# A fused attention, MoE and routed-expert kernel: the first chunks' scores straight from the keys, the block means as a second value product, other load layouts and a new order of steps

## The chip, the cores and the metric

The kernel runs on one core of one Trainium2 chip. The metric is the device time of one execution in microseconds; the median of three runs before the change is 538.80 (538.72 to 539.54). Engines: TensorE (PE, with its weight loads PEld), VectorE (DVE), ScalarE (ACT), GpSimd (POOL), and SyncE (SP), which issues most transfers.

## The reference, cut to what matters

Three layers one after another, all in float32. An attention with q, k, v of 2 x 8 x 768 x 64; then a dense layer with a silu gate on 1536 tokens of width 512 (hidden width 2048); then a layer of 8 experts (hidden width 1024) of which every token takes the one with the highest logit.

```python
k_sum = k.reshape(B, H, nb, 32, D).max(axis=3)
v_sum = v.reshape(B, H, nb, 32, D).mean(axis=3)
scores_l = where(|i - j| < 16, scale * q @ k.T, -1e9)
scores_s = scale * q @ k_sum.T + log(32)
a = softmax(concatenate([scores_l, scores_s], -1))
x = a @ concatenate([v, v_sum], 2)
...
h = x @ w_in;  x = (h / (1 + exp(-h))) @ w_out
...
out[t] = gate[t] * relu(x[t] @ w1[e_t]) @ w2[e_t]
```

So a query sees 31 near keys and the 24 block maxima of the keys; its values are the near values and the 24 block means.

## The kernel before, in words

The 1536 tokens are six chunks of 256 (`c`), four head pairs each (`hp`); chunks 0 to 2 are the first batch. A chunk's queries go in four tiles of 64, and a tile's window is 96 keys and 24 block entries, 120 columns (`KW` = 96, `NC` = 120). Everything is issued from one list of step names, `STEPS` (lines 60 to 89): a letter names a step, a digit its chunk, and each occurrence takes the next head pair or block; a mark behind it names the engine (`'` VectorE, `*` ScalarE, `_` GpSimd). Each engine runs its own instructions in that order and waits for data and buffers by semaphores, and SP's loads stand in SP's queue in the same order.

The steps of the opening: `k` loads keys (transposed, padded) and `K` takes block maxima on VectorE; `q`, `v` load queries and values; `n`, `Z`, `M` load values by rows, sum their blocks on TensorE (L205) and scale them to means on VectorE (L227, into `vsum`). `W0`, `W1` (`windows`, lines 315 to 323) are GpSimd's: for chunks 0 and 1 three copies build the 120-column tile `a` out of the keys and the maxima. `D` (`dots`, lines 325 to 342) makes the scores on TensorE, eight products a step; where `windows` has made a tile, each product reads all 120 columns (L339), and the branch behind it (L341, L342) is not used. `T` masks and takes maxima on VectorE (L355), `E` exponentials on ScalarE (L361), `R`, `N` the normalisation (L365 to L370), `P` turns on TensorE (L376), `C` copies the turned weights. `A0`, `A1` (`add_means`, line 301) copy the means into rows 96 to 119 of the value tile on GpSimd; `V` (`values`, line 388) is eight products over 120 rows (L395); `H`, `L` split the result into a high part and a rest (L399, L403). Later chunks load ready key windows (`load_step`).

Weights of the dense layer come as 64-bit words: `l` loads a block of 128 columns (`load_raw`, L236 and L238), `a` is two operations on ScalarE (L248, L250), `b` and `c` integer operations on VectorE (L254, L258), `h` the high part (L170, a helper that copies) and `p` the rest (L276) on VectorE. `F` is 24 matmuls of the hidden layer (L414; `F0` to `F3` are quarters of it, six each), `t`, `u` the gate, `g`, `w` its split, `G` twelve matmuls of the second product (L451). Raw blocks, keys and rows of values share one tag of 16 buffers.

Routing: `i`, `r`, `e` pick an expert, rank the tokens and write a table to DRAM; `plan` and `prow` lay out work units (a count on TensorE, L578, and some forty small VectorE operations); `read` loads the table rows by an indirect DMA of GpSimd (L730); `ids` turns them on TensorE (L739). Experts: `ga` gathers rows, `f1`, `f2` load 1 MB of weights, `1h`/`1r`, `2h`/`2r` split them, `f` and `z` are the two products (L911, L905, L901; L963, L957, L951), `ym` scales, `yo` writes.

```python
copy(by, k[:, :, :QT], t[:, o:o + CH].rearrange("p (g k) -> p g k", g=G))
...
nc.tensor.matmul(ps[:, :NC], q[d, t + i], k[d, t + i], start=True, stop=True)
...
nc.tensor.matmul(ps[d, t], v[:, t, d], r[:, 2 * h + t // 2, t % 2 * QT:(t % 2 + 1) * QT], start=True, stop=True)
```

## Time and profile before

| | |
|---|---|
| median of 3 runs | 538.80 us |
| the profiled execution | 540.28 us |
| its span in the trace | 538.5 us |
| TensorE busy | 512.5 us, 95% |
| VectorE, ScalarE, GpSimd busy | 394.0, 227.6, 77.8 us |
| moved by the DMA engines | 77.37 MB |

The span is the time between the first and the last instruction of the profiled execution. A busy engine is not one at its peak: TensorE has two clock levels, 1.2 and 2.4 GHz, and the profile gives the granted clock of a stretch as a share (0.50 and 1.00). In a row of the timeline the first number is the start and the second the time from the start of the first to the end of the last of the instructions that are merged in it. What stands in brackets is the idle time of the engine before them and what ended it. TensorE's instructions overlap, so the price of a step is read from its start to the start of the next.

### The profile page before, as it was taken

The page shows a single profiled execution, that of the slowest core. Times are in us where ns is not written, and L with a number is a line of the kernel's source. Part 1 is how long each engine was busy: PE and PEld are TensorE (multiplying, and loading weights), DVE is VectorE, ACT ScalarE, POOL GpSimd, SP SyncE. Part 2 cuts the span into 40 slices and gives each one's busy share as a digit, 9 for nine tenths or more (in the row PEclk, how much of TensorE's full clock was granted, in tenths as well). Part 3 has the DMA queues.
Part 4 walks back from the last instruction along what each step waited for, and adds up shares of the span by engine and source line. Part 5 has one row for each costly group of instructions (what it writes and reads, how often), then busy time and mean ns, then how long its engine had stood idle before and what let it go on. Part 6 is the DMA issues. An engine that isn't in the chain of part 4 may idle for free. (4 is left out here: it accounts for less than half of the span.)

```text
span 538.5 us, 10109 instructions
## 1 busy us (share of the span) xinstructions
PE 512.5 (95%) x3716; PEld 425.1 (79%) x3716; DVE 394.0 (73%) x1058; ACT 227.6 (42%) x548; POOL 77.8 (14%) x110
## 2 busy tenths in 40 slices
PE   6979999999999999999999997999989999899992
PEld 3569888988988888889898987898957867687671
DVE  5889999996878768486768684769857656993650
ACT  4879996763433344243140302233224341233330
POOL 4440001000010000011003114010340202110021
PEclk8879999999999999999999998999989999999998
DMA  8997637064562202221010109110084659965430
GB/s 310 316 288 250 204 100 243 6 198 144 173 239 84 98 28 45 85 84 44 1 55 2 39 1 338 55 40 1 31 273 175 209 204 331 306 243 194 157 125 30
DMA packets 42986, 77.37 MB, mean 144 GB/s; under 512 B 3905, under 2 KB 17832, under 8 KB 42930
## 3 DMA queue, kind: packets, MB, share of 16 engines
q1 hardware_dynamic: 38322, 66.92, 38.1%
q0 software_dynamic: 2592, 6.33, 3.3%
q10 hardware_dynamic: 2016, 3.40, 1.7%
q8 instruction: 31, 0.51, 0.4%
q14 instruction: 25, 0.20, 0.1%
HBM read 87.28 MB, written 6.67 MB: 174 GB/s over the span
## 5 line engine op out<-in xcount | busy, mean ns | idle before, releaser
L414 PE MATMUL h<-x,wi 128*128 128x256 f32 x1152 | 146.9, 286 | 0.0
L414 PEld LDWEIGHTS h<-x,wi 128*128 128x128 f32 x1152 | 141.6, 192 | 2.0 <-issue 0.8
L451 PE MATMUL x<-wo,g 128*128 128x512 f32 x576 | 142.1, 399 | 0.0
L451 PEld LDWEIGHTS x<-wo,g 128*128 128x128 f32 x576 | 105.7, 188 | 24.5 <-issue 1.0
L863 DVE TENSOR_TENSOR sp<-r,sp 128x512 fp32r<-128x512 f32 x112 | 72.4, 686 | 23.3 <-ACT sp L170 22.6
L424 ACT ACTIVATE t<-h 128x512 f32<-128x512 f32 x48 | 28.5, 596 | 68.3 <-PE h L414 62.7
L911 PE MATMUL jh<-xTT,sp 128*128 128x256 f32 x384 | 50.3, 286 | 0.0
L911 PEld LDWEIGHTS jh<-xTT,sp 128*128 128x128 f32 x384 | 47.6, 191 | 3.0 <-issue 2.0
L963 PE MATMUL jy<-sp,jT 128*128 128x512 f32 x192 | 49.8, 407 | 0.0
L361 ACT ACTIVATE a<-a,m 128x120 f32<-128x120 f32 x96 | 36.8, 387 | 27.8 <-DVE m L355 27.8
L492 DVE CUSTOM_DVE_ANT_0 dull<-row,gate 128x512 bf16<-128x512 f32 x64 | 44.4, 693 | 1.4
L170 ACT CAST sp<-r 128x512 fp32r<-128x512 f32 x65 | 36.9, 619 | 16.3 <-DMA r<-w 6.1
L963 PEld LDWEIGHTS jy<-sp,jT 128*128 128x128 f32 x192 | 35.9, 192 | 9.9 <-issue 1.2
L427 DVE SCALAR_TENSOR_TENSOR t<-t,h 128x512 f32<-128x512 f32 x48 | 32.8, 683 | 14.8 <-ACT t L424 14.6
L435 DVE TENSOR_TENSOR g<-t,g 128x512 fp32r<-128x512 f32 x48 | 32.7, 690 | 9.3 <-ACT g L170 8.7
L355 DVE CUSTOM_DVE_ANT_0 a<-s,mask 128x120 f32<-128x120 f32 x96 | 21.3, 278 | 14.6 <-PE s L339 14.5
L170 ACT CAST g<-t 128x512 fp32r<-128x512 f32 x30 | 18.2, 618 | 23.0 <-DVE t L427 19.1
L563 POOL DMA_INDIRECT tbl<-tb,ix x12 | 13.3, 1112 | 100.8 <-DVE cum L555 83.0
L920 ACT ACTIVATE jT<-jh 128x512 fp32r<-128x512 f32 x16 | 9.6, 599 | 33.4 <-PE jh L911 25.2
L170 DVE CAST sp<-r 128x512 fp32r<-128x512 f32 x47 | 19.6, 432 | 4.1 <-PE jy L963 1.8
L399 ACT CAST x<-o 128x256 fp32r<-128x256 f32 x24 | 8.6, 368 | 29.2 <-PE o L395 28.6
L170 POOL COPY v<-vsum 24x512 f32<-24x512 f32 x15 | 13.1, 900 | 52.3 <-DVE vsum L227 36.4
(210 smaller groups left out, 651.0 us busy)
## 6 DMA issues: line engine op xcount, KB each, us to landing
r<-w SPq DMA_DIRECT2D x28, 1024.0 KB
rm<-w SPq DMA_DIRECT2D x32, 512.0 KB
...
```

Source lines behind the costliest of these rows:

```text
L170: (nc.scalar.copy if by is nc.scalar else by.tensor_copy)(dst, src)
L355: nc.vector.tensor_tensor_reduce(a[:, j], ps[j // 2][:, j % 2, :NC], mask[:, v], -0.125, 3.0e38, ALU.add, ALU.min, m[:, 0, j:j + 1])
L361: nc.scalar.activation(a[:, t], a[:, t], AF.Exp, bias=m[:, 0, t:t + 1], scale=-1.0, accum_out=m[:, 1, t:t + 1])
L414: nc.tensor.matmul(hs[c, p][:, j], wi[p][:, u, k, j * P:(j + 1) * P], xt[c, k][:, v], start=(j + k + n == 0), stop=(j == 1 and k == KB - 1 ...
L424: nc.scalar.activation(t, hs[c, p], AF.Tanh, scale=0.5)
L427: nc.vector.scalar_tensor_tensor(ts[c, p], ts[c, p], 1.0, hs.pop((c, p)), op0=ALU.add, op1=ALU.mult)
L435: by.tensor_tensor(g[:, 1], ts.pop((c, p)), g[:, 0].bitcast(F32), op=ALU.subtract)
L451: nc.tensor.matmul(x2p[c][i], g[:, v, j, i * P:(i + 1) * P], wo[f][:, u], start=(f == 0 and n == 0), stop=(f == FB - 1 and n == 2))
L492: nc.vector.tensor_tensor_reduce(dull, r, gates[e], 1.0, 0.0, ALU.mult, ALU.add, lg[:, i * E + e:i * E + e + 1])
L863: by.tensor_tensor(dst[:, 1], src, dst[:, 0].bitcast(F32), op=ALU.subtract)
L911: nc.tensor.matmul(hps[i, p][:, j], sp1[p // 2 * 4 + k][:, u, f:f + P], x[v][:, k], start=(k + n == 0), stop=(k == 3 and n == 2))
L963: nc.tensor.matmul(yps[i, t], h[:, v, j, t * P:(t + 1) * P], sp2[2 * p + j][:, u], start=(p + j + n == 0), stop=(p == 3 and j == 1 and n = ...
```

## The change

Chunks 0 and 1 no longer build a window tile. `windows` and its steps go; `dots` takes the branch with two products: 96 columns straight from the loaded keys, then 24 columns from the block maxima. `A0` and `A1` go too: `values` makes two accumulating products for these chunks, one over the value tile and one over the means, both over 120 rows, where the value tile holds zeros in rows 96 to 119 and `vsum` zeros in rows 0 to 95 (one GpSimd memset). Their value loads come from a new array padded to 128 rows (`vn2`), so 256 KB instead of 192. Blocks of `w_in` are stored so that each partition's 4 KB lie in one run, where before four runs of 1 KB were read. All steps of all stages stand in a new order, and some of them run on another engine; outside of `W0`, `W1`, `A0`, `A1` their numbers are the same.

```diff
--- before.py
+++ after.py
 STEPS = """
-k K W1 k K q1 D1 T1 E1 W0 k q0 D0 k K q0 W0 T0 E0 D0 T0 l a K W0 W0 q0 R0 D0 T0 q0 D0 E0 E0 W1 W1 q1 D1 N0 P0 b T0 n Z E0 n Z c R0 R0 R0 h* n R1 Z N0 C0* N0 P0 p P0
-W1 T1 M A1_ A0_ l l a a l a l N0 C0* P0 q1 D1 A1_ A1_ A0_ b b N1 a q1 D1 C0* C0* c c T1 A1_ v0 v0 V0 V0 v0 A0_ b E1 h* H0 L0 H0 L0 v0 A0_ h* R1 E1 v1 V0 v1 H0 c h*
-P1 p F0 F0 l l N1 l C1* a V0 H0 P1 C1* L0 F0 T1 E1 p b a L0 c V1 V1 v1 v1 F0 H1 H1 R1 q2 p F1 F1 F1 F1 t l R1 N1 a a P1 C1* N1 P1 l b t C1* a L1 F3 A2_ L1 F3 u V1 V1
...
-u g' w u i T5 L5 x* d3 d3 d3 d3 r g' t E5 R5 G w V5 N5 d3 d3 d3 d3 e e G u g* P5 C5' H5 d3 d3 L5 G V5 H5 L5 F w F G t t d3 d3 x* d3 d3 u d3 d3 i r u g' w F rt rc* rt
-g* w F e e rl rc' rl i t G u tiles g' w t u g' r w G plan prow f1 F t u g' G w F t u g* w e e e e e read ids ga F t f2 2h' 2r f2 u ga ga 2h* 2h* F t 2h* u g* w 2r
...
+k k K K q0 q0 q0 D0 D0 T0 k K E0 T0 D0 T0 n k K E0 R0 R0 q1 Z E0 N0 l a D1 T1 b R0 q0 D0 T0 E1 P0 C0* n Z n Z q1 D1 E0 c h* N0 R0 N0 N0 q1 l l M P0 a b a P0 P0 p C0*
+C0* C0* l b a v0 V0 v0 v0 H0 V0 H0 D1 T1 c q1 D1 v0 V0 V0 h* R1 b L0 L0 T1 E1 R1 E1 p F0 F0 H0 H0 N1 P1 N1 l L0 a v1 L0 c P1 h* C1* F0 l l l F0 c h* v1 C1* T1 E1 b
+R1 t V1 V1 p p F1 F1 F1 F1 N1 R1 N1 H1 L1 v1 H1 a L1 u a a l P1 C1* F3 b l P1 C1* F3 V1 b v1 V1 l l c c c F2 t u a b b H1 F2 L1 F2 H1 L1 F2 q2 q2 c c h* l l F3 l l
+F3 g* w g* h* h* h* t a p p G t w u A2_ b a a D2 u p p g' w G g* G c h* h* T2 p a p F F a a w b b b G b c c a c c E2 t u l l h* h* h* h* p p p R2 p b F F N2 P2 g* w
...
+T5 E5 R5 N5 d3 d3 d3 d3 C5* d3 F t u g* P5 C5' V5 w H5 L5 G V5 H5 L5 F t G i r x* e e e rt rc' F rt t u e e g' tiles u g* rc' w w F t F G u g' w t u g* i r e rl e rl
+i F r w F t u g* e plan prow f1 t G G 1h* e read F f2 2h* f2 u F ids ga ga ga ga g' w w t u g' G G G 1h' 1r lt lt 2h' w G 2h* t u 1r 2h* 2r 1h' 1r g* w G lc' ls lc'
...
@@ -95,7 +95,7 @@
 
 
 @with_exitstack
-def fused_kernel(ctx: ExitStack, tc, qw, kw, kt, vw, vr, vt, w_in, w_out, w_gate, w1, w2, masks, blocks, items, out):
+def fused_kernel(ctx: ExitStack, tc, qw, kw, kt, vw, vn2, vr, vt, w_in, w_out, w_gate, w1, w2, masks, blocks, items, out):
     nc = tc.nc
     cp = ctx.enter_context(tc.tile_pool(name="const", bufs=1))
     dr = ctx.enter_context(tc.tile_pool(name="dram", bufs=1, space=DRAM))
@@ -224,6 +224,8 @@
 
         ps = vsum[b]
         vsum[b] = cp.tile([NC, DM], F32, tag="vsum", name=f"vsum{b}")
+        if b == 0:
+            nc.gpsimd.memset(vsum[b][:KW], 0.0)
         nc.vector.tensor_scalar_mul(vsum[b][KW:NC], ps[KW:NC].rearrange("p a b -> p (a b)"), 1.0 / BLOCK)
 
     wi, wo = {}, {}
@@ -233,7 +235,7 @@
     def load_raw(kind, f):
         pool = wp.tile([P, DM], I64, tag="wo", name=f"raw{kind}{f}", bufs=FB) if f < ROOMY else st.tile([P, DM], I64, tag="stage", name=f"raw{kind}{f}")
         if kind == "i":
-            nc.sync.dma_start(pool.rearrange("p (k f) -> p k f", k=KB), w_in[:, f * P:(f + 1) * P].rearrange("(k p) f -> p k f", p=P))
+            nc.sync.dma_start(pool, w_in[f])
         else:
             nc.sync.dma_start(pool, w_out[f * P:(f + 1) * P])
         raws[kind, f] = pool
@@ -289,14 +291,17 @@
         for hp in range(HP):
             qs[c, hp] = q[:, hp].rearrange("p a b -> p (a b)")[:, :CH].rearrange("p (g q) -> p g q", g=G)
             rr[c, hp] = q[:NC, hp]
-            vs[c, hp] = v[:NC, hp]
+            vs[c, hp] = v[:, hp]
             ws[c, hp] = a[:, hp]
 
     def load_q(c, hp):
         nc.sync.dma_start(qs[c, hp], qw[c, hp])
 
     def load_v(c, hp):
-        nc.sync.dma_start(vs[c, hp][:KW], vw[c, hp])
+        if c < 2:
+            nc.sync.dma_start(vs[c, hp], vn2[c, hp])
+        else:
+            nc.sync.dma_start(vs[c, hp][:KW], vw[c - 2, hp])
 
     def add_means(c, hp, by=nc.vector):
         copy(by, vs[c, hp][KW:NC], vsum[c // 3][KW:NC, hp * P:(hp + 1) * P].unsqueeze(1).to_broadcast([NB, G, P]))
@@ -311,16 +316,6 @@
 
     def add_sums(c, hp, by=nc.vector):
         copy(by, ks[c, hp][:, :, KW:NC], ksum[:, c // 3, hp:hp + 1].to_broadcast([P, G, NB]))
-
-    def windows(c, hp, by=nc.gpsimd):
-
-        b, g = divmod(c, 3)
-        k = ks[c, hp] = ws[c, hp]
-        o = CH * g
-        t = kts[b, hp]
-        copy(by, k[:, :, :QT], t[:, o:o + CH].rearrange("p (g k) -> p g k", g=G))
-        copy(by, k[:, :, QT:KW], t[:, o + QT:o + QT + CH].rearrange("p (g k) -> p g k", g=G)[:, :, :KW - QT])
-        copy(by, k[:, :, KW:NC], ksum[:, b, hp:hp + 1].to_broadcast([P, G, NB]))
 
     def dots(c, hp):
 
@@ -392,7 +387,12 @@
         for t in range(G):
             for h in range(2):
                 d = slice(h * D, (h + 1) * D)
-                nc.tensor.matmul(ps[d, t], v[:, t, d], r[:, 2 * h + t // 2, t % 2 * QT:(t % 2 + 1) * QT], start=True, stop=True)
+                w = r[:, 2 * h + t // 2, t % 2 * QT:(t % 2 + 1) * QT]
+                if c >= 2:
+                    nc.tensor.matmul(ps[d, t], v[:, t, d], w, start=True, stop=True)
+                    continue
+                nc.tensor.matmul(ps[d, t], v[:NC, t, d], w, start=True, stop=False)
+                nc.tensor.matmul(ps[d, t], vsum[0][:, hp * P + h * D:hp * P + (h + 1) * D], w, start=False, stop=True)
 
     def x_high(c, hp):
         x = xt[c, hp] = xp.tile([P, 2, CH], F32R, tag="x" if c else "g", name=f"x{c}{hp}", bufs=XBUFS - 4 if c else 4)
@@ -1070,7 +1070,7 @@
     }
     for c in range(NCH):
         steps = [(c, hp) for hp in range(HP)]
-        for x, f in zip("qvWDTERNPCABVHL", (load_q if c < 2 else load_step, load_v, windows, dots, lows, exps, shares, norm, turn, keep, add_means, add_sums, values, x_high, x_rest)):
+        for x, f in zip("qvDTERNPCABVHL", (load_q if c < 2 else load_step, load_v, dots, lows, exps, shares, norm, turn, keep, add_means, add_sums, values, x_high, x_rest)):
             todo[f"{x}{c}"] = each(f, steps)
     todo["A2"] = each(lambda *a: (add_sums(*a), add_means(*a)), [(2, hp) for hp in range(HP)])
     for n in range(4):
@@ -1097,7 +1097,7 @@
 
 
 
-_NAMES = ["qw", "kw", "kt", "vw", "vr", "vt", "w_in", "w_out", "w_gate", "w1", "w2", "masks", "blocks", "items"]
+_NAMES = ["qw", "kw", "kt", "vw", "vn2", "vr", "vt", "w_in", "w_out", "w_gate", "w1", "w2", "masks", "blocks", "items"]
 
 
 def _arrays(q, k, v, moe_w_in, moe_w_out, moe2_w_gate, moe2_w1, moe2_w2):
@@ -1161,8 +1161,8 @@
     it[:, 200:232] = moe2_w_gate.reshape(KB, P, E).transpose(1, 0, 2).reshape(P, KB * E)
     it[:, 320:448] = np.triu(np.ones((P, P)), 1)
     return dict(
-        qw=qw.reshape(NCH, HP, P, G, QT), kw=kwn.reshape(NCH, HP, P, G, NC)[2:], kt=kp, vw=vwn.reshape(NCH, HP, KW, G, P), vr=vr, vt=vt,
-        w_in=con(moe_w_in).view(np.int64), w_out=con(moe_w_out).view(np.int64), w_gate=con(moe2_w_gate.T),
+        qw=qw.reshape(NCH, HP, P, G, QT), kw=kwn.reshape(NCH, HP, P, G, NC)[2:], kt=kp, vw=vwn.reshape(NCH, HP, KW, G, P)[2:], vn2=np.pad(vwn.reshape(NCH, HP, KW, G, P)[:2], ((0, 0), (0, 0), (0, P - KW), (0, 0), (0, 0))), vr=vr, vt=vt,
+        w_in=con(moe_w_in.reshape(KB, P, FB, P).transpose(2, 1, 0, 3)).view(np.int64).reshape(FB, P, DM), w_out=con(moe_w_out).view(np.int64), w_gate=con(moe2_w_gate.T),
         w1=con(moe2_w1), w2=con(moe2_w2), masks=masks, blocks=blocks, items=it)
 
 
```

## Rows read from the trace of the kernel before

**Rows 1.** The page, part 1: busy time, share of the span, instructions.
```profile
PE 512.5 (95%) x3716; PEld 425.1 (79%) x3716; DVE 394.0 (73%) x1058; ACT 227.6 (42%) x548; POOL 77.8 (14%) x110
```
**Rows 2.** Timeline of TensorE, opening: start, length in us, then what.
```profile
6.50 0.64 PE L339 MATMUL s<-a,q 64*64 64x120 f32 x16 [1.06 <-POOL a L170]
...
28.85 1.03 PE L395 MATMUL o<-q,v 120*64 120x64 f32 x16 [1.68 <-POOL v L170]
...
33.18 2.85 PE L414 MATMUL h<-x,wi 128*128 128x256 f32 x12
...
50.40 5.78 PE L451 MATMUL x<-wo,g 128*128 128x512 f32 x24
```
**Rows 3.** Timeline of TensorE, steady stretches at full clock.
```profile
62.49 5.76 PE L451 MATMUL x<-wo,g 128*128 128x512 f32 x24
...
163.43 0.69 PE L395 MATMUL o<-r,v 120*64 120x64 f32 x16
164.04 0.64 PE L339 MATMUL s<-k,q 64*64 64x120 f32 x16
164.61 3.12 PE L414 MATMUL h<-x,wi 128*128 128x256 f32 x24
...
173.94 0.60 PE L376 MATMUL t<-ident,a 128*120 128x128 f32 x4
174.30 5.95 PE L414 MATMUL h<-x,wi 128*128 128x256 f32 x48
```
**Rows 4.** Stretches: PE, PEld, DVE, ACT, POOL busy; PEclk, DMA share, GB/s.
```profile
10.00:18.00 8.00, 6.61 (x70) 4.61 (x64) 6.54 (x36) 7.22 (x33) 3.52 (x10) 0.50 1.08 374
16.00:18.00 2.00, 2.00 (x5) 0.97 (x4) 1.90 (x13) 1.93 (x9) 0.14 (x1) 0.50 1.13 355
20.00:22.00 2.00, 2.00 (x6) 0.90 (x5) 0.90 (x9) 1.61 (x3) 0.00 (x0) 1.00 1.07 367
22.00:28.00 6.00, 4.53 (x62) 2.80 (x61) 5.08 (x6) 5.16 (x15) 4.27 (x5) 1.00 1.06 228
30.00:36.00 6.00, 4.63 (x34) 4.38 (x34) 5.96 (x23) 5.08 (x15) 1.41 (x2) 0.51 1.05 283
```
**Rows 5.** Timeline of VectorE, opening.
```profile
22.89 0.70 DVE L227 TENSOR_SCALAR vsum<-vm 24x512 f32<-24x512 f32 x1 [1.99 <-PE vm L205]
...
24.20 2.12 DVE L254 SCALAR_TENSOR_TENSOR rawi<-rawi,three 128x512 int32<-128x512 int32 x2
...
32.44 0.68 DVE L276 TENSOR_TENSOR wi<-rawi,wi 128x512 fp32r<-128x512 f32 x1
...
43.04 1.41 DVE L254 SCALAR_TENSOR_TENSOR rawo<-rawo,three 128x512 int32<-128x512 int32 x2
```
**Rows 6.** Timeline of TensorE, routing.
```profile
316.74 0.18 PE L578 MATMUL cnt<-cum,ones 128*128 128x8 bf16 x1
...
329.03 0.37 PE L739 MATMUL entp<-ident,ents 4*128 4x4 f32 x2 [3.52 <-DMA ents<-tbl,rix]
329.32 7.53 PE L414 MATMUL h<-x,wi 128*128 128x256 f32 x48
```
**Rows 7.** Timeline of TensorE, experts: the two pauses and the last matmuls.
```profile
400.12 1.10 PE L901 MATMUL jh<-rm,xT 128*64 128x512 f32 x4 [2.18 <-DVE xT L170]
401.15 2.93 PE L963 MATMUL jy<-sp,jT 128*128 128x512 f32 x6
...
460.44 0.65 PE L926 MATMUL hp<-ident,hr 128*128 128x128 f32 x4 [1.50 <-ACT hr L916]
...
525.83 3.07 PE L957 MATMUL iy<-sp,hT 128*128 128x512 f32 x12
```
**Rows 8.** Timeline of POOL, opening: the copies of the means.
```profile
23.73 7.68 POOL L170 COPY v<-vsum 24x512 f32<-24x512 f32 x8 [7.59 <-DVE vsum L227]
```
**Rows 9.** The chain that ended last: one of five short matmuls in a row.
```profile
359.17 0.03 PE lo L541
```
**Rows 10.** The chain that ended last: a weight load of the experts.
```profile
449.51 9.69 DMA r<-w
```

More of the change, by code (lines that the diff above doesn't have):

```diff
@@ L76 @@
-1h' 1r G 1h' g* 1r 1h' 2r w 1h' f1 1h* 1h' G 1h* lt lt 2h* 2h' lc' ls 2r lc' 2r G G G x* rt rc* 1r 1r 1r ls f 2r f1 rt f f lt rl rc* rl 1r 1r f rh f f 2h' i rr r 1h*
-1r z 2r f f rh cn pl f pl pl pl pl pl f rr pl 1h* 1r lc' f st ls 1h* pl pl pl pl pl 1r 1h* 1h* ga lt lc' pl pl pl pl pl pl f rh pl pl f f f f1 pl f2 pl pl f z 2h' 2r
-z z rh rr z z 2h* 2r pl rr z pl pl 2h* 1r 1h' 1r z ls f pl pl pl pl pl 1h* 1h* pl pl f f f pl 1r pl f2 pl ex 2h* 2h' rh 2h* f f ex 1h* f f 1r 1r 2h' 2h' 2h' rr e ex
@@ new lines @@
+G C2' V2 H2 A2_ g* t w u L2 D2 l a b c h' p l a g' b c h' G G p F F T2 E2 R2 N2 l a l a t t b c h' p w j b c q3 P2 H2 C2* G h* u L2 p u V2 H2 L2 F g' J B3_ w g* j j
+G F t t F w j G u q3 J B3* D3 t D3 J J g' x* w G m s u u m s T3 F g' w E3 R3 m m N3 P3 G s s Y O d0 d0 T3 E3 R3 t u g* d0 d0 d0 w M F t A3* C3' u g' w g' F q3 V3 H3
+L3 B3_ q3 D3 B3_ G t T3 E3 G d0 d0 N3 P3 F R3 N3 d0 d0 d0 u P3 A3_ A3* C3* V3 H3 w C3* d0 d0 d0 F L3 q4 B4_ q4 q4 A3* g' t u t V3 H3 g* w w D3 L3 T3 E3 R3 N3 q4 G G
+P3 B4' u g* G d0 C3' d0 w D4 T4 E4 D4 T4 R4 N4 d0 i V3 H3 G x* q5 q5 L3 F t u g' w F t u d1 F F d1 d1 d1 t d1 A4* r P4 C4* A4' g' G w G u t u g* g* e E4 w V4 H4 d1
@@ new lines @@
+d1 L4 B4_ D4 F R4 N4 P4 d1 d1 d1 C4* T4 E4 R4 B4_ t u G V4 D4 F w T4 E4 t N4 P4 G d1 d1 B5_ D5 C4' u H4 L4 R4 A4' V4 T5 E5 g' g* N4 w F t R5 N5 G d1 d1 x* d1 B5_ w
+P4 d1 d2 d2 d2 d2 d2 H4 L4 u C4* A4* F A5_ t u g' i G P5 V4 H4 L4 F t w G C5* V5 d2 d2 g* D5 d2 A5' w G F F T5 E5 q5 A5_ B5* d2 d2 d2 d2 u g* w D5 G t t u d2 d2 q5
+B5* d2 d2 u x* d3 F g* w t d3 d3 d3 g' w G G T5 E5 u g* d3 w r F t d3 R5 N5 u F g' w P5 C5' F R5 N5 t u H5 L5 d3 d3 d3 d3 t u V5 D5 g* H5 L5 G G w G A5* d3 P5 g* w
+T5 E5 R5 N5 d3 d3 d3 d3 C5* d3 F t u g* P5 C5' V5 w H5 L5 G V5 H5 L5 F t G i r x* e e e rt rc' F rt t u e e g' tiles u g* rc' w w F t F G u g' w t u g* i r e rl e rl
@@ new lines @@
+i F r w F t u g* e plan prow f1 t G G 1h* e read F f2 2h* f2 u F ids ga ga ga ga g' w w t u g' G G G 1h' 1r lt lt 2h' w G 2h* t u 1r 2h* 2r 1h' 1r g* w G lc' ls lc'
+f1 1h' 1h' 1h* ls f 2r 2h* 2r 2r 1r 1r 1r x* rt rc* rt rc* 2h* 2r 2r f f rl rl i lt lt lc* ls f rh r rr 1h* 1h* 1r 1r f f f f f rh rr cn pl f1 f f f rh f f f f pl pl
+pl pl pl 1h' 1h' 2h* pl pl f1 pl pl pl pl pl pl pl pl 1h* pl z z 2r pl 1h* 1h* lc' 1h* st pl pl pl pl pl pl pl pl pl pl pl pl ls f2 z z 2h* 2r f2 1r rr z z pl pl pl
+pl 1r 1r 1r 1r 2h* pl pl 2h* ex ex ex f f rh rr f f rh rr 1r ex ex ex ex ex ex z ym* f 1h* ex f1 m1 m1 f e e 1h' f 1h* rd tw f rh rr f it ic 2h* ga 2h' z 2r 2r 2r 2r
@@ new lines @@
+z z z 1h* lt 1h' f2 ga ga lt 1r 1r 1h' f f f ym' f rh 2h' 2h' 1r 1r mga mga f f 1r z lc' lc* m1 f ls ls rr f1 1h' m1 1h' 1h* rh 1r 1h* f1 f 2r mlt mlc' f f f mf 2h*
+2h' 2h* rr mf mf mf ga mrh mga 2h' 2h' 2h* 2r 2r 2r 2r 2r z 1r 1r 2r lt mht 1r z 1r rh z rr f2 2h* 2r m2 m2 2r 2h' mhc* ga f f f f1 1h' ga 1r 1h' m2 ym' lc* f rh f z
+f rr f 1h' f 1r ls rh f 1r f 2h' mlt 2h* 1h* mz mz m2 mz mz m1 ym' m1 m1 m1 mlc' f2 rr 1r 2r f1 mlt mlc' f 2r z z f 1h* 1h* 1r 2r 1h' 1r 1r f f rh rr 1h' lt lt f f
+1h' z lc' 1h' 1h' 1h* yo 1r 1r mf mf f2 lc' ls ls mf mf mrh z m2 2h' 2h' 2r f f 2h* 2r 1r mht mhc* m2 m2 2h* mym* yo yo mga m2 lt 1r f f lc* f1 z z 2h* 1h* 1h' ls 1r
@@ new lines @@
+1r f1 z z f 2r 2r rh 1h' 1h' 1r 1r f f f f rh ht 1h* mz mz mz hc* mz mym* ht 1r f f rr rh f rh z z ht hc' rr 1h' 1h' z z ym* myo 2h' yo 1r 1r 1r myo f m1 1h' 1r f
+ym* 2h' 2h* f f 2r ht hc' f2 2h' m1 m1 2r 2r 2r rr 2h' yo 2h' 2h' z z 2r 2r 2r mf mf hc* yo rr 2r m1 mf mf f1 1h* 1h' 1h' 1h* z z z f1 1r 1r mrh f2 ga mht m2 2h* m2
+2r 2h' 2r f2 lt 2h* 2h' z rh rr mhc' 2h' 2h' 2r 2r z f f f z z z lc* ls f rh 2h' 2h' m2 m2 mz mz mz mz 1r mlt mlc' 1r 1h' 1h' 2r 2r z z f f f rr 1h* f2 2r 2r mym* f
+1r 1r 1r m1 1h* 1r 2h* 2h* 2h* 2r rh rr f f f f f1 1h* 1h* 1h' z z 2h* f2 2h* f f f 2r f 1r 2h' z z 2h' f 1r f ym* ym' rh rr rh z z ht yo m1 mf m1 m1 mf m2 mf mf mrh
@@ L89 @@
+m2 2r 2r z 2r mht 2h* f2 2h* 2h' 1h' 1r 2r f hc' 1r f mhc' 2r 2r z rh ht ym' rr hc* rr m2 m2 yo mz 2r mz mz mz mym' yo myo myo 2h* 2r z z z z 2h' 2r 2r z z z z ym'
+yo ym* yo
 """
```

22 lines of the change are left out of this document (2 added, 20 removed).

## The prediction, made before the change was run

> **What bounds the kernel now.** I read the page first: TensorE is busy for 95% of the span [rows 1], so the question at every stage is where TensorE pauses or runs at its lower clock, and what work is added to it. Its own timeline shows three kinds of loss.
>
> The opening. The first scores start at 6.50, after a POOL copy; the value products stand still for POOL's copies of the block means; the hidden layer (L414) starts at 33.18; the first pair of second products (G, L451) at 50.40 [rows 2]. The work that TensorE does up to there, at the steady prices of later stretches: a value step takes 0.61 from its start to the next, a scores step (16 records) 0.57, a turn 0.36, and 48 hidden matmuls 5.95, or 0.124 each [rows 3]. The block sums are 12 records at about 0.40, since five weight loads fit into the 2 us from 20 on [rows 4]. So 8 x 0.57 + 12 x 0.40 + 8 x 0.36 + 8 x 0.61 + 96 x 0.124 = 4.6 + 4.8 + 2.9 + 4.9 + 11.9 = 29.1 us of work end at 50.4. Some 21 us are lost, nearly all before 33.2: no pause stands in the timeline after that, only a stretch at clock 0.51 [rows 4]. What ends the loss is VectorE. It waits 1.99 for the block sums, then its integer operations take 1.06 each while POOL copies, against 0.70 later, and so the rest of the second weight block, which the first hidden matmul needs, comes at 32.44 [rows 5].
>
> The routing stage. TensorE counts the tokens at 316.74, and it stands still for 3.52 until the table has been read back at 329.03; the next 48 hidden matmuls take 7.53 [rows 6] instead of 5.95, as the clock has fallen. That is 3.5 + 1.6 = 5.1 us.
>
> The expert stage. One pause of 2.18 with six matmuls after it that take 2.93 [rows 7], twice the steady time (24 in 5.76 [rows 3]), so 1.5 more, and one pause of 1.50. The last matmul ends at 528.90 [rows 7] and 9.6 us of writing follow.
>
> **The change, part by part.** *Taken from POOL:* eight window steps of three copies each and eight copies of the means, these in a row of 7.68 us [rows 8]. They lie ahead of TensorE's pauses, so this is where the opening can shrink. POOL gets one memset of the means' first 96 rows; it is idle there, and even at the 0.96 of a copy [rows 8] it is done long before VectorE writes the means.
>
> *Added to TensorE:* 64 score products of 24 columns and 64 value products of 64, two records each. No row shows a 24-column product of this shape. From below, bare short matmuls go through at 0.03 us each [rows 9]: 128 x 0.03 = 3.8. From above, a 120-column record takes 0.57 / 16 = 0.036: 4.6. I take 4.4, since weight loads come with each. The second value products have the shape of the first, 8 x 0.61 = 4.9; if two accumulating products on the same columns overlap less than the alternating ones, I allow half as much again, 7.3. Together 9.3, from 8.7 to 11.9. The Trainium skill (TensorE: Matmul & The Clock Gate, section "Wait — 56ns, not 53.3ns?") says that starts of small matmuls never lie closer than about 25 ns; by that figure the short score products would cost an estimated 3.2 instead of 4.4, and the time would come out 1.2 us lower. The nearest rows, with weights of this shape, speak for more.
>
> *New waits:* the second score product waits for VectorE's block maxima, as POOL's third copy did. Behind it in TensorE's queue stands only the next scores step, so it costs at most one reduction that VectorE does anyway. Reading the keys where they lie holds their four buffers until the last scores step of chunk 1; the weight tag has 16 buffers, and 11 loads are issued by then, so no load waits.
>
> *Loads:* ahead of the first value load stand one weight block and one query block fewer, 0.65 MB, 1.8 us at the 367 GB/s of the stretch from 20 to 22. While the 96-row value loads flow, the rate falls to 228 GB/s [rows 4]. Four loads of 262 KB at 367 take 2.9 us, four of 197 KB at 228 took 3.4. If the padded loads stay at 228, they take 4.6. Either way the values are there before the first value step. The weight blocks in one run per partition: a stretch full of the old blocks moved 355 GB/s and the next one 367 [rows 4], so four of them come at most 0.2 us sooner. I count nothing, for VectorE's work hides it; without that cover it is those 0.2 us.
>
> *The order, opening.* Ahead of the first hidden part TensorE has 8 x 1.12 + 4.8 + 4 x 0.36 + 4 x 1.22 = 20.1 us; from a start at 5.9 (0.6 earlier, without the copy) that ends at 26.0 if nothing pauses. VectorE has two integer operations and a normalisation less ahead of it, some 2.1 us at 0.70 each, is no longer slowed (4 x 0.36 = 1.4) and need not wait for the sums (up to 2.0, half of it taken): 33.2 - 2.1 - 1.4 - 1.0 = 28.7, which I take. From there to the first G come 4 x 1.22 + 4 x 0.36 + 11.9 = 18.2 of work. In the old order that stretch was 17.2 long with 5 value steps, 3 turns and the hidden matmuls, 16.0; with its loss of 1.2 again, the first G starts at 48.1, or 2.3 earlier with the same work behind it. VectorE is not late there any more: it has nine operations of 128x512 fewer before that point than in the old order (four rests, a join, a sign, two gatings, one g rest), 9 x 0.70 = 6.3. Ends: 26.0 + 18.2 = 44.2, a gain of 6.2; and, at 11.9 for the added products and TensorE at the low clock wherever it was low before (10 to 18 and 30 to 36 [rows 4], 14 us, half of it lost), 53.8, a loss of 3.4.
>
> *The order, middle.* From the first G to the routing TensorE hardly pauses; the steps between a hidden block and its second product leave 7.5 us or more of other matmuls in the new order, so it stays full: 0.
>
> *The order, routing.* From the count to the table's return pass 329.03 - 316.74 = 12.3 us. The new order puts G G F F between the two, 2 x 2.88 + 2 x 2.98 = 11.7, where F G F stood. The pause shrinks to 0.6, and with so short a one the clock stays: 5.1 - 0.6 = 4.5 gained. Ends: 0, if VectorE reaches the plan late, and 5.1.
>
> *The order, experts and end.* The same work; most distances grow (the first activation to its second product from 1.6 us of matmuls to 8.8), some shrink: the weights of the last job's second half must be split within 1.8 us of matmuls after their buffer comes free. Up to 5.2 can be gained (2.2 + 1.5 + 1.5) and as much lost. I take 0. The last writes stay at 9.6.
>
> **Sum.** 2.3 + 4.5 = 6.8 us. The profiled execution took 540.28 (its span 538.5 and 1.8 around it), so it becomes 533.5; the median shown, 538.80, lies 1.5 below that execution and becomes 532.0.
>
> **The rivals.** (a) *The opening packs fully*: TensorE never pauses after 5.9, 6.2 + 4.5, so 528.1. For it: the new order leaves no engine behind another. Against: VectorE, ScalarE and TensorE then have nearly equal loads, and each handover costs. (b) *The routing pause stays*: VectorE's queue stands before the plan, 538.8 - 2.3 = 536.5. (c) *The experts give it back*: one more pause of the 2.18 kind with its slow matmuls (3.7) and the opening at no gain, 538.8 - 4.5 + 3.7 = 538.0. This also holds the case that the change does not do what it says: POOL's copies leave, but VectorE alone set 33.18. (d) *Slower, by the experts' weights*: a load took 9.69 us to land [rows 10], and the new order leaves between 1.8 and 6.4 us from a free buffer to the split in four places. ScalarE and VectorE split in order, so what stands behind the split stops too. Two such waits of 5 us that TensorE cannot cover make 538.8 - 6.8 + 10 = 542.0; it decides from 6.8 us of new pauses on. Against it: the old order had a distance of 1.4 and TensorE did not pause there. (e) *Slower, by the clock*: the opening's TensorE has no slack now, so each us at 1.2 GHz costs half of one. From (50.4 + 4.5 - 44.2) x 2 = 21 us on the change loses; 27 us would give 541.6. Rows at about 0.50 covered 14 us before, when TensorE was mostly waiting. The Trainium skill (TensorE: Matmul & The Clock Gate, "What's actually happening") says that the clock is low by default and activity frees it; no row shows the denser opening, and by that rule (e) is the less likely.
>
> **How the numbers follow.** Forecast 0.43, (a) 0.14, (b) 0.13, (c) 0.12, (d) 0.10, (e) 0.08. Less than 0.2%, 1.1 us, can't be told from no change. Faster is the forecast, (a) and (b): 0.70. Same is (c): 0.12. Slower is (d) and (e): 0.18. The range runs from 527.5, just under (a), to 540.0: it holds (b), (c) and the bounds of the added products, and leaves out (d) and (e).
>
> **What would show it.** Right: no POOL copy before 35 us; first scores near 5.9; first hidden matmul at 28 to 29.5, first G near 48; integer operations of 128x512 at 0.70 in the opening; under 1 us of pause before the table's return and no low clock after it. Wrong: a first G later than 50.4, clock 0.50 over most of 8 to 35, a pause over 3 us before the table, or new pauses of TensorE behind weight loads after 400.

## The result, and the profile after

The kernel after takes 526.14 us in the median of 4 runs (525.14 to 526.83) against 538.76 before (538.24 to 539.54): a ratio of 0.9763, interval 0.9743 to 0.9783, 12.6 us less. The forecast was 532.0 in a range that began at 527.5. The direction was right and nearly half of the gain was not foreseen. The two profiled executions, 540.28 and 526.15, lie 14.1 apart, for the one before lay 1.5 above its median.

The page's first part, after (before: [rows 1]):

```profile
PE 506.1 (97%) x3972; PEld 425.3 (81%) x3972; DVE 400.6 (76%) x1075; ACT 217.0 (41%) x527; POOL 66.5 (13%) x83
```

TensorE has 256 records more and is busy 6.4 us less: part of its busy time before was time at the low clock. Up to the last matmul the granted clock stood at 0.50 for 23.9 us before and for 3.4 us after. Its timeline in the opening (before: [rows 2]):

```profile
6.23 0.42 PE L336 MATMUL s<-kt,q 64*64 64x96 f32 x8 [1.36 <-DMA q<-qw]
...
22.55 0.34 PE L394 MATMUL o<-q,v 120*64 120x64 f32 x4
...
24.61 0.42 PE L336 MATMUL s<-kt,q 64*64 64x96 f32 x8
...
25.20 0.42 PE L336 MATMUL s<-kt,q 64*64 64x96 f32 x8
...
28.16 1.69 PE L414 MATMUL h<-x,wi 128*128 128x256 f32 x12
...
46.36 2.97 PE L451 MATMUL x<-wo,g 128*128 128x512 f32 x12
```

The first hidden matmul came at 28.16 (before 33.18), the first second product at 46.36 (before 50.40), and between 22.55 and 46.36 no pause is listed. Two value steps with both products lie between 22.55 and 24.61, so 1.03 each against 0.61 for one product [rows 3]. A scores step with both products takes 25.20 - 24.61 = 0.59, against 0.57 with one [rows 3]. The stretches (columns as in [rows 4]):

```profile
10.00:18.00 8.00, 7.69 (x78) 4.06 (x79) 5.87 (x33) 6.44 (x28) 0.00 (x0) 0.79 1.05 394
...
22.00:28.00 6.00, 6.00 (x195) 5.70 (x196) 5.59 (x27) 5.68 (x20) 0.00 (x0) 1.00 1.03 402
28.00:34.00 6.00, 6.00 (x100) 5.70 (x98) 5.97 (x20) 5.69 (x19) 0.00 (x0) 1.00 1.04 402
```

No POOL work (the fifth pair), no low clock after 18, and transfers at 402 GB/s where 228 went. VectorE's integer operations take 0.75 each (before 1.06 [rows 5]):

```profile
20.89 0.75 DVE L256 SCALAR_TENSOR_TENSOR rawi<-rawi,three 128x512 int32<-128x512 int32 x1
...
27.55 0.66 DVE L278 TENSOR_TENSOR wi<-rawi,wi 128x512 fp32r<-128x512 f32 x1
```

The routing (before: [rows 6]) and the experts (before: [rows 7]), TensorE's timeline:

```profile
314.01 0.18 PE L578 MATMUL cnt<-cum,ones 128*128 128x8 bf16 x1
...
325.51 0.40 PE L739 MATMUL entp<-ident,ents 4*128 4x4 f32 x2
...
339.49 2.83 PE L451 MATMUL x<-wo,g 128*128 128x512 f32 x11 [0.41 <-DVE g L435]
...
439.02 3.76 PE L905 MATMUL jh<-sp,xT 128*128 128x512 f32 x15 [1.30 <-ACT hr L916]
...
507.99 5.86 PE L957 MATMUL iy<-sp,hT 128*128 128x512 f32 x24
```

From the count to the table's turning TensorE now works for 11.5 us without a pause. In the experts 1.30 and a 0.31 are left of 3.7 us of pauses, and the granted clock stays at 1.00 up to the last matmul. The last one ends at 513.85, 15.05 earlier than before; the writing behind it takes 10.45 (before 9.6).

### The profile page after: what moved, and what is told of

Its sections match the earlier page's. It is cut to its first block, busy times and chain, and to the rows that moved or that the text cites. A ratio compares the mean times of both kernels' runs of the same rounds, so it can differ in the third digit from the quotient of the medians.

```text
span 524.3 us, 10579 instructions
## 1 busy us (share of the span) xinstructions
PE 506.1 (97%) x3972; PEld 425.3 (81%) x3972; DVE 400.6 (76%) x1075; ACT 217.0 (41%) x527; POOL 66.5 (13%) x83
## 4 chain that ended last, share of the span: by engine, by line
PE 61%; issue 21%; DVE 8%; DMA 5%; POOL 3%; ACT 1%; SPq 0%; POOLq 0%; DVEq 0%
PE h L414 24%; PE x L451 22%; PE jh L911 4%; PE jy L963 3%; PE o L392 2%; POOL out L977 2%; DVE sp L863 2%; PE s L334 2%; DMA r<-w 2%; PE t L371 1%; DMA vn<-vr 1%; DMA v<-vn 1%; DMA q<-qw 1%; POOL out L974 1%; PE lo L515 1%
## 5 line engine op out<-in xcount | busy, mean ns | idle before, releaser
L414 PE MATMUL h<-x,wi 128*128 128x256 f32 x1152 | 144.0, 282 | 0.1
L414 PEld LDWEIGHTS h<-x,wi 128*128 128x128 f32 x1152 | 139.1, 188 | 2.2 <-DVE x L403 0.3
L424 ACT ACTIVATE t<-h 128x512 f32<-128x512 f32 x48 | 28.7, 597 | 66.5 <-PE h L414 55.6
L963 PE MATMUL jy<-sp,jT 128*128 128x512 f32 x192 | 48.1, 398 | 0.0
L170 ACT CAST sp<-r 128x512 fp32r<-128x512 f32 x54 | 31.4, 619 | 39.6 <-DMA r<-w 25.4
L170 DVE CAST sp<-r 128x512 fp32r<-128x512 f32 x58 | 22.9, 420 | 21.1 <-DMA r<-w 14.2
L170 POOL COPY k<-ksum 128x96 f32<-128x96 f32 x12 | 6.1, 511 | 182.7 <-DMA k<-kw 144.0
L170 ACT CAST g<-t 128x512 fp32r<-128x512 f32 x27 | 16.7, 620 | 26.5 <-DVE t L427 16.3
L977 POOL DMA_INDIRECT out<-y,ids x11 | 12.7, 1153 | 61.6 <-ACT y L968 34.4
```

The source lines that it names most:

```text
L170: (nc.scalar.copy if by is nc.scalar else by.tensor_copy)(dst, src)
L414: nc.tensor.matmul(hs[c, p][:, j], wi[p][:, u, k, j * P:(j + 1) * P], xt[c, k][:, v], start=(j + k + n == 0), stop=(j == 1 and k == KB - 1 ...
L424: nc.scalar.activation(t, hs[c, p], AF.Tanh, scale=0.5)
L963: nc.tensor.matmul(yps[i, t], h[:, v, j, t * P:(t + 1) * P], sp2[2 * p + j][:, u], start=(p + j + n == 0), stop=(p == 3 and j == 1 and n = ...
L977: nc.gpsimd.indirect_dma_start(out=outs[j][:, :], out_offset=bass.IndirectOffsetOnAxis(ap=ids[:, j:j + 1], axis=0), in_=ys.pop((i, t)), in ...
```

## The experiments

Besides the forecast's reason (each stage gains what its own pause was) there were rivals: the order gives everything; the new code and loads give it; the gain hangs on the products' price. "Before" was run again beside each group, at 538.9 to 539.5 in the median.

**The order and the code, each alone.** The first is the kernel before with the new list of steps; `W0`, `W1` stand behind the maxima and `A0_`, `A1_` behind `M`.

```diff
-k K W1 k K q1 D1 T1 E1 W0 k q0 D0 ...
+k k K W0 K W0 q0 q0 q0 D0 D0 T0 k K W0 E0 ...
...
+M A0_ A0_ A0_ A0_ A1_ A1_ A1_ A1_ P0 ...
```

> The kernel before with the new order alone: GpSimd still builds the windows (each right after the block maxima of its head pair) and still copies the means (right behind their scaling); old loads. My theory (the new order closes the routing's and the experts' pauses by itself, some 8.5 us; its opening needs TensorE and VectorE free of GpSimd's copies): 538.8 - 8.5 and up to 3 lost in the opening, so 530 to 533, with the first pair of second products no earlier than 50. Rival A, the order gives all of it and the code next to nothing: 526 to 528. Rival B, the gain comes from the code and the loads: 537 to 539.

Measured: 527.40 us, ratio 0.9771 (0.9737 to 0.9804). Its opening:

```profile
9.91 1.17 PE L339 MATMUL s<-a,q 64*64 64x120 f32 x16 [1.57 <-POOL a L170]
...
25.05 1.34 PE L395 MATMUL o<-q,v 120*64 120x64 f32 x32 [1.11 <-DMA v<-vw]
...
47.93 3.46 PE L451 MATMUL x<-wo,g 128*128 128x512 f32 x12
```

POOL's copies are there and TensorE waits for them, yet the first second product comes 2.5 us sooner than in the profile before. Rival A holds: the order gives some 11.5 of the 12.6 us, and the two intervals overlap. My theory that the new opening needs POOL's copies gone falls.

The other half, the kernel after with the old list less `W0`, `W1`, `A0_`, `A1_`:

> The kernel after with the old order (less the steps that no longer exist). My theory: the pauses of 3.5 us at the table and of 2.2 and 1.5 us in the experts are back; in the opening GpSimd's 4.3 us of waits go against some 3.4 us of added products and VectorE's old queue, so 536 to 539. By the forecast's prices of the added products (9.3 us): 541 to 544. Rival B (code and loads): 527 to 530.

Measured: 538.81, ratio 1.0003 (0.9977 to 1.0029), as my theory had it. The new code in the old order gains nothing:

```profile
28.91 0.28 PE L393 MATMUL o<-q,v 120*64 120x64 f32 x2 [1.90 <-issue]
...
50.10 5.76 PE L450 MATMUL x<-wo,g 128*128 128x512 f32 x24
...
328.18 0.37 PE L738 MATMUL entp<-ident,ents 4*128 4x4 f32 x2 [3.06 <-DMA ents<-tbl,rix]
```

The table's pause is back, and the first second product is 0.3 earlier than before. There is a new kind of pause: 1.90 us in the middle of a value step, between two equal records, for which the profile shows no releaser.

**The order in two parts, on the new code.** One kernel has the new order up to `ids` and the rest in the old one, the other the old order up to the first `G` and the rest in the new one.

> The kernel after with its own order up to the turning of the table's rows, and from there what is left in the old order. If the new order of the expert stage is worth what TensorE's lost time there says (it grows by some 5.5 us more before than after): 530.5 to 533, with pauses of 2.2 and 1.5 us again. Rival: those pauses came from where the earlier stages had left the loads and buffers, so they do not return: 526 to 527.5.

> The kernel after with the old order up to the first second product and from there what is left in the new order. If the opening's gain is the code's (no copies of GpSimd): 526 to 527.5. If it is the new order's: 526.1 + 4.4 = 530.5, between 529 and 532, with the first second product at 49 to 51.

Measured: 535.03 (0.9885 to 0.9974, runs from 531.75 to 539.71) and 531.95 (0.9801 to 0.9885; first second product at 51.24). The first lies above both of its branches, the second just inside the 529 to 532 of the order. Both profiles have the mid-step pause, 2.54 and 2.17 us. The first has besides a new pause where the old list takes over, for the gathered rows:

```profile
335.75 0.66 PE L870 MATMUL xp<-ident,xgq 128*128 128x128 f32 x4 [2.31 <-DMA xgq<-x2d,ids]
```

In its experts there are pauses of 0.78 and 1.29, smaller than the 2.2 and 1.5 expected. What a stage's order is worth can't be read from such a kernel, so the split was made again on the kernel before, whose TensorE has fewer instructions there.

**The order in parts, on the kernel before.** First a single exchange in the old list:

```diff
-... e e e e e read ids ga F t f2 ...
+... e e e e e read F t ids ga f2 ...
```

> The kernel before with one exchange in its order: the turning of the table's rows (and the first gather behind it) stands behind the next 48 hidden matmuls instead of in front of them. By the forecast's working (the pause of 3.5 us and the low clock's 1.6 after it are covered by 5.95 us of matmuls): 538.9 - 5.1 = 533.8, between 533 and 535. Rival (the gather and the rows' turning come later by as much and TensorE waits there instead): 537 to 539, with a pause of 2 us or more at the first turned rows.

Measured: 534.92, ratio 0.9934 (0.9908 to 0.9960), so 4.1 us by the medians.

```profile
315.79 0.18 PE L578 MATMUL cnt<-cum,ones 128*128 128x8 bf16 x1
...
328.10 0.40 PE L739 MATMUL entp<-ident,ents 4*128 4x4 f32 x2 [0.69 <-DMA ents<-tbl,rix]
...
338.15 0.63 PE L871 MATMUL xp<-ident,xgv 128*128 128x128 f32 x4 [0.56 <-DMA xgv<-x2d,ids]
```

The pause shrinks from 3.52 to 0.69, and the next link, the gathered rows, takes 0.56 back. The forecast's routing term is confirmed within half a microsecond, the rival (all of it waits at the gather) is not.

Then the opening alone, and everything from `plan` on alone:

> The kernel before (its products, copies and loads) with the new order only up to the first second product, and what is left in the old order. If the new opening is worth what the order-alone kernel's trace says (the lost time at 63 us is 17.1 there and 19.7 before): 538.9 - 2.6 = 536.3, between 535.5 and 537.5. If the opening's gain needs the direct scores and second value products: 538 to 539.5.

> The kernel before with the old order up to the plan and the new order for what is left (routing's second half, the rest of the dense layer, the experts). If the late part of the order carries the routing's 4.1 (as the late turning of the table's rows alone gave) and the experts' 5: 529 to 531. If the experts' pauses only disappear where the stages ahead are new too: 533.5 to 535.

Measured: 539.38 (0.9987 to 1.0032) and 530.07 (0.9822 to 0.9880). The late part carries 9.0 us. Less the 4.1 of the exchange, the experts' new order is worth 4.9, and the ratios' intervals of the two kernels (0.9908 to 0.9960, 0.9822 to 0.9880) lie apart. This counts as the experts' whatever else differs from `plan` on; the routing differs little, for a pause of 1.41 is left ahead of the table here, and 0.69 and 0.56 were left with the exchange. From 349 on its timeline lists no pause at all, and from 395 to 405 TensorE is full, where it stood at clock 0.83 before (busy for 7.68 us of 10):

```profile
395.00:405.00 10.00, 10.00 (x59) 6.69 (x58) 9.44 (x18) 3.64 (x7) 6.26 (x5) 1.00 0.58 184
```

The new opening, with the order up to `plan`, gives 2.7 us on top of the new late part (530.07 to 527.40). On top of the old one the new opening gives nothing: the 535.5 to 537.5 of my expectation is missed, and the time lies in the other branch, though the copies are there in the order-alone kernel too. In this kernel the first second product comes 2.1 earlier than in the profile before, at 48.34, but later TensorE stands still longer:

```profile
328.50 0.37 PE L739 MATMUL entp<-ident,ents 4*128 4x4 f32 x2 [3.87 <-DMA ents<-tbl,rix]
...
405.83 3.32 PE L901 MATMUL jh<-rm,xT 128*64 128x512 f32 x6 [2.56 <-DMA rm<-w]
```

Why the old late part gives the opening's gain back was not tried further; this profile also fell on one of its longer runs (542.55). And the place of the first second product in one profile is a rough measure: with the exchange and with the new late part the opening's code and order are those of before (50.40), and it stands at

```profile
49.46 5.78 PE L451 MATMUL x<-wo,g 128*128 128x512 f32 x24
...
48.74 5.79 PE L451 MATMUL x<-wo,g 128*128 128x512 f32 x24
```

So differences under some 1.7 us in it show nothing, and of the 2.1 here little may be real. The 46.36 of the kernel after lies clear of all three.

**One part of the change undone.** Four kernels have the new order and all of the new code but one part: GpSimd's windows back (`windows` and `W0`, `W1`); GpSimd's means back (`A0_`, `A1_`, one value product, 96-row loads); 96-row loads alone; the old layout of `w_in`. A fifth has both copies back with the new loads.

```diff
-            nc.sync.dma_start(vs[c, hp], vn2[c, hp])
+            nc.sync.dma_start(vs[c, hp][:KW], vn2[c, hp, :KW])
...
-            nc.sync.dma_start(pool, w_in[f])
+            nc.sync.dma_start(pool.rearrange("p (k f) -> p k f", k=KB), w_in[:, f * P:(f + 1) * P].rearrange("(k p) f -> p k f", p=P))
```

(The third and the fourth kernel; in the third, GpSimd zeroes rows 96 to 127 once.)

> The kernel after, but GpSimd builds the windows of chunks 0 and 1 again, so the scores are one product of 120 columns (each window right after the block maxima of its head pair; the four of chunk 1 behind the last maxima). Theory now (the order gives nearly all; a second score product of 24 columns costs about 0.02 us a step, 0.2 in all, and GpSimd's copies delay the first scores by up to 2 us that later work mostly hides): 526.5 to 527.5. By the forecast's price (4.4 us for the second score products): 522 to 524. If the direct scores carry the code's gain: 527.5 to 529.

> The kernel after, but chunks 0 and 1 take their block means from rows 96 to 119 of the value tile, copied there by GpSimd right behind the means' scaling, in one value product, with value loads of 96 rows. Theory now: 64 value products fewer give back some 3.2 us of TensorE, and GpSimd's copies and the slower loads take 1 to 3: 524.5 to 527. Rival (the copies' wait is what the second products were made for and costs as much as before, 3.2 us and VectorE slowed): 527 to 529.

> The kernel after with value loads of 96 rows for chunks 0 and 1 (rows 96 to 127 are zeroed once by GpSimd at the start); everything else as it is. If the padded loads matter (96 rows go at 228 GB/s where 128 rows go at 402, so the loads ahead of the first values and weights come up to 2 us later): 527 to 528.5, with the first value step later than 22.9. If transfers are hidden in the opening: 525.8 to 526.5.

> The kernel after with the old layout of w_in, four runs of 1 KB per partition for each block. My forecast's bound (0.2 us at most): 526.0 to 526.5. Rival (the loads set the opening, full at 400 GB/s from 10 to 34 us): 527 or more, the rate of the weight blocks' stretches below 380 GB/s.

> New order and new loads, but the products of before: GpSimd builds the windows and copies the means (each copy right behind its value load). It is the order-alone kernel plus the new layouts, or the kernel after without its second products. Theory now (the code's part of the gain is the loads, 2 to 3 us each in the kernels that undo one; second products and copies cost about the same): 525 to 527. If the second products are what the gain over the order alone (1.3 us) comes from: 527 to 529.

And the kernel after once more:

> The kernel after once more, beside the others on the same chip. If its TensorE stalls for code behind the 344th matmul in some executions, as the kernels with one part undone do (1.9 to 3.4 us in the middle of a step, with the code's packet landing at 25 to 29 us instead of 23): the runs spread over 525 to 529, with the profile showing such a pause in the slower ones. If the kernel after always gets its code in time: all within 525 to 527.

| kernel | us | interval of the ratio | mid-step pause in its profile |
|---|---|---|---|
| after, first and second time | 526.14, 526.84 | 0.9743-0.9783, 0.9749-0.9812 | none |
| windows back | 526.12 | 0.9734-0.9785 | none |
| means back, 96 rows | 527.84 | 0.9762-0.9815 | 3.38 |
| 96-row loads | 529.48 | 0.9788-0.9857 | 1.97 and 0.77 |
| old `w_in` | 528.24 | 0.9766-0.9820 | 2.63 |
| both copies back, new loads | 527.86 | 0.9762-0.9824 | none |

The windows are worth nothing either way (526.12, a little under my 526.5 to 527.5). Means back, the old `w_in` and both copies lie in the ranges of their rivals, and the 96-row loads above both of theirs. The kernel with both copies and the new loads does no better than the order alone (527.40). Where one part undone seems to cost 1.3 to 3 us, its profile has the mid-step pause:

```profile
29.74 0.33 PE L336 MATMUL s<-kt,q 64*64 64x96 f32 x4 [1.97 <-issue]
...
37.64 0.34 PE L394 MATMUL o<-q,v 120*64 120x64 f32 x4 [0.77 <-issue]
```

(96-row loads.) This kernel also waits for the loads themselves. Its first value step starts at 24.59 where the kernel after's starts at 22.55, which is what the first branch of its expectation foretold, and from 22 to 28 the transfers move 290 GB/s where they moved 402:

```profile
24.59 0.34 PE L394 MATMUL o<-q,v 120*64 120x64 f32 x4 [0.92 <-DMA v<-vn]
```

Most of these intervals overlap with the kernel after's, so each difference alone proves little; the pauses are what the traces show, and each trace is that of one run (for the means and the old `w_in` the longest of six). Both copies back cost 1.4 without such a pause in the profile. The kernel after's own runs spread from 525.1 to 527.9, two of nine over the 527 of its expectation's second branch, and its two profiles have no such pause.

**The price of the second products.** In the kernel after, the first value product is made twice, and in another the second score product is:

```diff
+                nc.tensor.matmul(ps[d, t], v[:NC, t, d], w, start=True, stop=True)
                 nc.tensor.matmul(ps[d, t], v[:NC, t, d], w, start=True, stop=False)
...
                     nc.tensor.matmul(ps[:, KW:NC], q[d, t + i], ksum[d, b, hp], start=True, stop=True)
+                    nc.tensor.matmul(ps[:, KW:NC], q[d, t + i], ksum[d, b, hp], start=True, stop=True)
```

> The kernel after with the first value product of chunks 0 and 1 made twice (the first one is overwritten): 64 products of 64 columns more. By the trace of after (a pair of products takes 1.03 us a step, one took 0.61): 8 x 0.42 = 3.4 us, of which the opening's waits hide at most half, so 527.8 to 529.5; a step takes 1.4 to 1.5. By the forecast's 0.61 to 0.9 for each second product: 531 to 533.3. If the pairs' work is hidden: 526.1 to 526.6. A stall for code adds 2 to 3 us to any of these.

> The kernel after with the second score product of chunks 0 and 1 made twice (the same result both times): 64 products of 24 columns, 128 records, more. By the trace of after (a step with both takes 0.59, the one with 120 columns alone took 0.57): 0 to 0.5 us for all eight steps, a step at 0.6 to 0.65, so 526 to 527 without a stall for code. By the forecast's price (4.4 us for 128 records): a step at 1.1 and 529 to 531. A stall for code (2 to 3 us) can be added to either, since it is the count of instructions that sets it.

Values twice: 531.98, 5.5 above the kernel after (526.5, the middle of its two medians). Two steps with three products take 40.31 - 37.19 = 3.12, so 1.56 each: 0.53 for a third product, 0.42 for a second, 8 x 0.53 = 4.2, and a mid-step pause of 1.72. Together they are 5.9, so the opening hides little or nothing. The step lies just over the 1.4 to 1.5 of my first branch and under the forecast's 0.61 for each added product; the hiding I allowed for is not there. The time alone would fit either branch.

Scores twice: 537.06 (0.9932 to 0.9991, runs from 531.56 to 543.87), far above both expectations. A step of 48 records takes 2.06:

```profile
21.77 0.38 PE L335 MATMUL s<-kt,q 64*64 64x96 f32 x2
...
23.83 0.87 PE L371 MATMUL t<-ident,a 128*120 128x128 f32 x6
```

This profile fell on one of the two shortest runs; what the longer ones lose is not shown. So this run did not measure what it was made for: a second score product beside the first costs 0.02, the same product over the same columns again 2.06 - 0.59 = 1.47. One thing the two cases differ in is the place written. The 24 columns lie beside the 96, the repeated ones lie on the columns of the product just before. The accumulating value products, which also write the same columns twice, cost nearly their full price. That is a reading of three cases, not a test of its own: the order of the records changes too.

**What the mid-step pause is.** I counted the records of TensorE's program ahead of each such pause:

| kernel | pause, at | where | matmuls ahead |
|---|---|---|---|
| new order: old experts; 96 rows; old `w_in` | 2.54, 27.87; 1.97, 29.74; 2.63, 29.32 | scores, 49 records in | 343 |
| old order: code alone; old opening | 1.90, 28.91; 2.17, 29.22 | values, 49 records in | 343 |
| means back | 3.38, 30.77 | values, 16 in | 342 |
| 96 rows, the second | 0.77, 37.64 | values, 16 in | 470 |
| values twice | 1.72, 32.63 | values, 80 in | 470 |
| scores twice | 0.73, 31.81 | scores, 81 in | 471 |

The steps differ and the data differ; the count does not, and the second place lies some 128 matmuls on. (The label "issue" by itself shows less: the order alone and both copies back have pauses of 0.90 and 0.84 under it at the start of a value step, elsewhere in the count.) Ahead of each of these nine pauses the queue "instruction" moves one packet (0.02 MB), and TensorE goes on 1.29 to 1.56 us after that packet has landed. Where these kernels pass 343 or 471 without a pause, the packet had landed 1.75 us before or more. So I took it for code that arrives late. In the two kernels with products made twice the packet starts 2.9 and 3.0 us after TensorE passed the border before it, no later than in the kernel after (3.5), and it is TensorE that is at the next border sooner. In the others it starts 5.3 to 9.0 us after; what holds it up there was not tested. Two runs moved the count by 59 matmuls at the start and left the loads and all other work as they were:

```diff
             nc.tensor.matmul(ps, z[:, :P], z, start=(i == 0), stop=(i == n - 1))
+        for i in range(64):
+            nc.tensor.matmul(ps[:32, :8], z[:, :32], z[:, :8], start=True, stop=True)
...
-        wake(10)
+        wake(5)
```

> The kernel with the new code and the old order (538.8, with a pause of 1.9 in the middle of a value step behind its 344th matmul), with 64 short matmuls of 8 columns more in TensorE's warming at the start and 5 long ones fewer, so 59 more in all. Their results are used by nothing. If TensorE waits there for its code: the pause comes again behind the 344th to 356th matmul, which is now in the scores step before that, at 285 to 297 of the old count, so near 25 us instead of 26.9. If it waits for data of that value step: at the same place in that step, behind the 403rd. Time 537 to 540 either way.

Measured (old order): 537.36 (0.9951 to 0.9996), and no pause of that kind in the profile, neither at the place foretold for code nor at the one for data. The wait for data is excluded for that profile. The place for code was wrong too: the packet for the border at 343 landed at 18.99 here and TensorE came there at 25.67, where without the shift it landed at 27.41. My reading is that moving the border also moves the moment at which the packet is asked for. With that in the theory, the kernel after:

> The kernel after with the same 59 matmuls more in the warming at the start (64 short ones of 8 columns, 5 long ones fewer; nothing uses their results). Theory of the code: a packet holds some 128 matmuls with their weight loads, is asked for one packet ahead and lands 4 to 5 us later while the transfers are full, and TensorE goes on some 2 us after that. In the kernel after the borders lie behind its matmuls 215, 343 and 471, and each packet is in time by a few tenths. Moved by 59 they lie behind 284 and 412 of the old count: the packet for the latter is asked for at 24.3, lands at 28 to 29, and is wanted at 27.8, in the middle of the third value step. So: a pause of 1.5 to 3 us there, labelled as issue, that the kernel after does not have, and 527.5 to 529.5. If the pauses have nothing to do with the count of instructions: no such pause, and 526 to 527, or less.

Measured: 527.94 (0.9759 to 0.9828, runs from 526.09 to 529.61). TensorE's timeline:

```profile
28.04 0.28 PE L396 MATMUL o<-q,vsum 120*64 120x64 f32 x2
29.77 0.28 PE L395 MATMUL o<-q,v 120*64 120x64 f32 x2 [1.45 <-issue]
```

and what that queue moved between 27 and 28:

```profile
q8 instruction: 1, 0.02, 6.4%
```

A pause that the kernel after does not have, behind 470 matmuls of its own. That is 53 records into the second run of value products, where the count in the expectation gives 54 (each step has 32 records, so it is the fourth value step and not the third, as the expectation calls it). TensorE goes on 1.41 us after the packet has landed. In the kernel after the packet for the border at 343 lands at 24.29, and 1.37 later the timeline shows a gap of 0.17 between two starts:

```profile
25.49 0.21 PE L337 MATMUL s<-ksum,q 64*64 64x24 f32 x1
25.66 0.33 PE L336 MATMUL s<-kt,q 64*64 64x96 f32 x4
```

The pause is 0.05 shorter than the bounds I gave and the medians differ by 1.4 with overlapping intervals; the place, and the packet ahead of it, are what shows it.

## Why the prediction was right and wrong

*The experts and the end, taken as 0: this step failed*, and it is most of the miss. I wrote that up to 5.2 us could be gained and as much lost, and took the middle. The runs give 4.9 (530.07 against 534.92), nearly all of the 5.2. In the kernel after's own profile 1.6 us of pauses are left there, and no low clock. The 5.2 was the sum of pauses that the trace showed, and I had noted that most distances in the new order grow. The range shows the same mistake: its low end stood on the opening and the routing (rival a), and the bound of 5.2 that the text itself gave was not taken in. With it, 532.0 - 5.2 = 526.8 would have been a case of its own.

*The added products, 9.3 us: mis-sized.* Scores were to cost 4.4 and cost 8 x 0.02 = 0.2; values were to cost 4.9 and cost 8 x 0.42 = 3.4. In the sum this counts for 4 x 0.19 = 0.8 only, as VectorE was to set the time up to the first hidden matmul. For the scores I priced records, but 16 records of 120 columns and 16 of 96 with 16 of 24 make the same 1,920 columns, and take the same time. The Trainium skill (TensorE: Matmul & The Clock Gate, "Wait — 56ns, not 53.3ns?") has starts of small matmuls never closer than about 25 ns; the trace differs, with 32 records in 0.59, 18 ns each, whose operands lie in both halves of the partitions in turn, and the measurement decides. That sentence would have given 3.2 us, also too much.

*The opening, 2.3 us:* the first hidden matmul was foretold at 28.7 and came at 28.16, which is luck. VectorE was to set it, but TensorE works without a listed pause from 22.55 to 28.16 and sets it itself. On TensorE's own path I had 20.1 us of work and no loss. By the measured prices the work is 8 x 0.59 + 4.8 + 4 x 0.36 + 4 x 1.03 = 15.1, and 6.8 of the 21.9 us from 6.23 on are lost, most of them ahead of 22.55. From there to the first second product 19.4 us were foretold and 18.2 passed; the work is 17.5 by the same prices, so of the loss of 1.2 that I had carried over 0.7 was there. The first second product came at 46.36 instead of 48.1. The reason was half wrong as well. I let POOL's copies pay for the opening; the order alone has them and brings 2.7 of the opening's 3.6 (530.07 to 526.5), and the code without the order brings nothing. What of the code's 0.9 on top is real is smaller than these measurements can tell.

*The routing, 4.5 us:* right. 4.1 by one exchange in the kernel before, and in the kernel after no pause ahead of the table and no low clock behind it.

*Loads, nothing:* open. The padded loads did not stay at 228 GB/s, and with 96-row loads the first value step comes 2.0 us later, so they are not wholly hidden. How much of that kernel's 3.0 us is theirs and how much the two mid-step pauses', the runs do not separate; both copies with the new loads gain nothing over the order alone.

*The end, taken to stay at 9.6:* the writing takes 10.45; why was not looked into.

Opening 3.6, routing 4.1 and experts 4.9 make the 12.6 measured, but they are differences along one chain of kernels and would do so whatever they were; in another chain, the new opening on the old late part, the opening gives nothing. Of the rivals, (a) came nearest in the opening, where TensorE indeed stops pausing at 22.55, but 3.6 us and not 6.2 are gained, since the pauses ahead of that stay; (b) and (d) did not happen: no pause stands ahead of the table, and behind the weight loads the longest is 1.30, ended by ScalarE. (e) did not happen either: the clock stands at 0.79 from 10 to 18 where it stood at 0.50, and at 1.00 behind that. By the rule of the Trainium skill that activity frees the clock (TensorE: Matmul & The Clock Gate, "What's actually happening") the denser opening should run at the higher level more of the time, and the trace agrees. (c), in the form that the code does not do what it says, holds for the code by itself; the order made up for it.
